# Reading the moving columns of the feed-forward products alternately from the left and the right half

## The chip, the core and the metric

The kernel runs on one core of one Trainium2 chip. The metric is the device time of one launch in microseconds (us); of the kernel before there are three runs, with a median of 897.61 us (897.53 to 898.24). Beside these times there is one profiled execution, whose trace is read below. All arithmetic happens on the core; the host only lays the input arrays out.

## The reference

Eight sequences of 576 tokens with eight heads of 64 features go through an attention that looks only inside chunks of 64 tokens. The result, 4608 tokens by 512 features, goes through a gated feed-forward part with 1536 hidden features:

```python
def _attn_ref(q, k, v):                       # each (8, 8, 576, 64), chunk = 64
    scores = scale * np.matmul(q_c, k_c.transpose(0, 1, 2, 4, 3))
    scores = scores - np.max(scores, axis=-1, keepdims=True)
    attn = np.exp(scores)
    attn = attn / (np.sum(attn, axis=-1, keepdims=True) + 1e-09)
    out = np.matmul(attn, v_c)

def _moe_ref(x, w_gate, w_val, w_out):        # x (4608, 512)
    g = x @ w_gate                            # (512, 1536)
    silu = g * (1.0 / (1.0 + np.exp(-g)))
    val = x @ w_val
    return (silu * val @ w_out).astype(np.float32)
```

Tokens are independent of each other in the feed-forward part: whatever order the 4608 rows are worked in, each gives the same row of the output.

## The kernel before

**Tiling.** The 4608 tokens are worked in 9 groups of 512 (`N`), the 512 input features in 4 blocks of 128 (`NK`), the 1536 hidden features in 12 blocks `f` of 128 (`NF`). A group's attention output lies in SBUF with features on the 128 partitions and the 512 tokens along each partition. So the products of the feed-forward part all have one shape. A weight block of 128 x 128 is loaded into the TensorE array, and 512 columns are streamed past it into one PSUM bank. The streamed operand is called the moving operand here. In the gate and value products it is a group's tokens (`x`, `xh`, `xl`); in the output product (`project`) the array holds 128 hidden-layer tokens and the moving operand is the 512 columns of a block of the output weights (`both`, `two`).

**Precision.** Each float32 factor is split in an upper and a lower part, both of the type float32r (names ending in h or hi, and l or lo), by a cast on ScalarE and a subtraction on VectorE (`split`, L62 and L63). Each product is then three matmuls: lower times upper, upper times lower, upper times upper. The weights arrive as 64-bit floats and are narrowed on the chip (`class Narrow`): a ScalarE instruction reads the high 32-bit words of the pairs (L80), another the low words (L87), so both step by two words. `class Out` does this for the output weights, 512 columns per block `f`.

**Order of the work.** Groups 0 and 1 come first, together with the narrowing of the weights. Their blocks 0 to 5 are plain products (`some`, L475); the later blocks combine two groups in a scheme of seven products instead of eight (`seventh`, L863). The narrowed weights and their sums are written to device memory on the way. Group 2 follows with plain products. Groups 3 and 4, 5 and 6, 7 and 8 are then worked in pairs with seven products per block (`gated_pair`), reading the weights back from device memory block after block. The gated hidden block `h` is split again and multiplied by the output weights (`project`, L538 to L540), which adds up in four PSUM banks, one per 128 tokens, over all 12 blocks. After the last block, ScalarE scales each bank into `o_sb` and a DMA on SP's queue writes the 128 rows to the output (L553, L554). The order of instructions on TensorE, ScalarE and VectorE is that of the program text (`manual_schedule`); attention steps of later groups are put between the feed-forward steps by tables of callbacks (`middle`, `behind`, `bursts`).

**Operand addresses.** Every moving operand of the lines L475, L538 to L540 and L863 is a run of 512 consecutive 4-byte words in each partition. One other line streams 512 columns: L664, which subtracts the row maxima from the scores of the first two groups. Its moving operand is a short row of maxima, each repeated 64 times:

```python
nc.tensor.matmul(ps, minus, top[:, h].broadcast_to(list(ps.shape)), start=False, stop=True,
                 skip_group_check=True)
```

Of the kernel before, what the change touches and what calls it, by code (L numbers as in the profile page):

```python
# [8 lines left out]
F32 = mybir.dt.float32  # L9
F32R = mybir.dt.float32r  # L10
U32 = mybir.dt.uint32
I32 = mybir.dt.int32
U64 = mybir.dt.uint64
AF = mybir.ActivationFunctionType
# [3 lines left out]
P = 128  # L18
C = 64
B, H, S, D = 8, 8, 576, 64  # L20
NT = B * S
# [5 lines left out]
T = 4  # L27
N = T * P
NB = NT // N
# [4 lines left out]
def attn_then_gated_ffn(ctx: ExitStack, tc: tile.TileContext, qk, v, wgv, wo, out):  # L34
    nc = tc.nc
# [15 lines left out]
    minus = const.tile([P, P], F32R, name="minus")  # L51
    nc.scalar.activation(minus, ident, AF.Copy, scale=-1.0)

    def keep_warm(n):

        ps = ps_gv.tile([P, P], F32, name="unread", tag="ps_gv")
        for _ in range(n):
            nc.tensor.transpose(ps, ident, ident)
# [6 lines left out]

    w_hi, w_lo, wo_raw, w_both = [], [], [], []

    class Narrow:


# [6 lines left out]


        def scale(self):
            nc.scalar.activation(self.t, self.high.bitcast(F32), AF.Prelu, scale=2.0 ** -111, alpha=2.0 ** 32)  # L80

        def shift(self):
            nc.vector.tensor_scalar(out=self.ti, in0=self.ti, scalar1=3, scalar2=None, op0=ALU.logical_shift_left)


        def below(self):
            nc.scalar.activation(self.units, self.low.bitcast(U32), AF.Copy, scale=2.0 ** -29)  # L87

        def join(self):
            nc.vector.tensor_tensor(out=self.ti, in0=self.ti, in1=self.units, op=ALU.add)  # L90
# [84 lines left out]
    def moved(i):  # L175
        return f"w{(i + EARLY) % NF}"
# [47 lines left out]
    class Out(Narrow):  # L224
# [14 lines left out]
        def scale(self):  # L239
            wo_raw.append(const.tile([P, 2, DM], F32, name="wo", tag=f"wo{self.f % 2}")[:, 0])  # L240
            super().__init__(self.mine, wo_raw[self.f], hp.tile([P, DM], F32, name="o_sb", tag="o_sb"))
            super().scale()


# [226 lines left out]
    def some(ps, a, f, g, which, first=True, last=True):  # L471
        for k, i in which:
            w = (w_hi, w_lo, w_hi)[i][f][:, g, k]
            x = a.x[k // 2][i == 0][:, k % 2]
            nc.tensor.matmul(ps, w, x, start=first and (k, i) == which[0], stop=last and (k, i) == which[-1])  # L475

    def out_weights(f):
        both = wp.tile([P, 2, DM], F32R, name="both", tag="wo")
        split(wo_raw[f], both[:, 0], both[:, 1])
        if f % 2 == 0:  # L480
            o = store.tile([P, 2, 2, DM], F32, name=f"o{f}")
            kept_o[f], kept_o[f + 1], two_o[f // 2] = o[:, 0], o[:, 1], o
        out_now[f] = both
        return both[:, 0], both[:, 1]
# [6 lines left out]
    def out_again(f, pool=wp, tag="wo"):  # L491
        both = pool.tile([P, 2, DM], F32R, name="both", tag=tag)
        recent[:] = [nc.sync.dma_start(out=both.bitcast(F32), in_=kept_o[f]).ins]
        return both[:, 0], both[:, 1]
# [7 lines left out]
    def product(a, f, g):  # L502
        ps = ps_gv.tile([P, N], F32, name="ps_gv")
        some(ps, a, f, g, IN_TURN)
        return ps
# [24 lines left out]
        return a, f, hh, hl  # L530

    def project(parts, wo_f, which=range(T)):
        (a, f, hh, hl), (woh, wol) = parts, wo_f
        if not hasattr(a, "o"):
            a.o = [ps_o.tile([P, DM], F32, name="ps_o") for _ in range(T)]
        for t in which:
            ts, o = slice(t * P, (t + 1) * P), a.o[t]
            nc.tensor.matmul(o, hl[:, ts], woh, start=f == a.steps[0], stop=False)  # L538
            nc.tensor.matmul(o, hh[:, ts], wol, start=False, stop=False)  # L539
            nc.tensor.matmul(o, hh[:, ts], woh, start=False, stop=f == a.steps[1])  # L540
            if f == a.steps[1]:

                pool, tag = (hp, "o_sb") if t % 2 == 0 else (ld, "v_t")
                o_sb = pool.tile([P, DM], F32, name="o_sb", tag=tag)
                r = a.b * N + t * P

                halves = 2 if r + P == NT else 1
                for i in range(halves):
                    m = slice(i * DM // halves, (i + 1) * DM // halves)
                    if i:  # L550
                        nc.vector.tensor_scalar_mul(o_sb[:, m], o[:, m], 2.0 ** -8)
                    else:
                        nc.scalar.activation(o_sb[:, m], o[:, m], AF.Copy, scale=2.0 ** -8)  # L553
                    nc.sync.dma_start(out=out[r:r + P, m], in_=o_sb[:, m])  # L554

    pending = []

    def lag(parts, wo_f):

        if pending:  # L560
            project(*pending.pop())
        if parts is not None:
            pending.append((parts, wo_f))
# [21 lines left out]
    w, o = up[0], down[0]  # L585
# [36 lines left out]
    class Product:  # L622
# [4 lines left out]
        def add(self, *which):  # L627
            for w in which:
                self.left -= 1
                some(self.ps, *self.at, [w], first=self.left == 3 * NK - 1, last=not self.left)  # L630
# [68 lines left out]
    for a, qs in ((a0, q0[0] + q0[1]), (a1, q1[0] + q1[1])):  # L699
# [16 lines left out]
        L13 w1u  # L716
    """
    keep_warm(15)
    for do in opening.split():
        if do[0] == ".":  # L720
            keep_warm(int(do[1:]))
        elif do[0] in "gvw":
            getattr(weights[do[:-1]], steps[do[-1]])()
        elif do[0] in "GV":
            if do[0] not in products:
                products[do[0]] = Product(a0, 0, "GV".index(do[0]))
            products[do[0]].add((int(do[3]), int(do[4])))
        elif do[0] == "e":
            a0.exchange(v0[int(do[1])][:, 1], values[int(do[1])][1], nc.scalar.copy)
        elif do == "H0":  # L730
            h0 = silu(products["G"].ps)
        elif do == "Q0":
            times(h0, products["V"].ps)
        else:
            b, i = int(do[1]), int(do[2])
            pairs = do[0] in "STCUL"
            getattr(couples[b, i // 2 if pairs else i], do[0])(i if pairs else int(do[3:] or 0))
# [4 lines left out]
    w = up[1]  # L742
# [16 lines left out]
    wo_f = out_weights(0)  # L759
# [52 lines left out]
    for f in range(1, SEVEN):  # L812
        w, o = up[f + 1], down[f]
# [32 lines left out]
        wo_f = out_weights(f)  # L846
# [11 lines left out]
    def seventh(ps, x, factors, i, first):  # L858
        which, q = FACTORS[i]
        w = [t.rearrange("p (i k m) -> p i k m", i=4, m=P)[:, q] for t in factors[which]]  # L860
        for k in range(NK // 2):
            for n, (u, v) in enumerate(((0, 1), (1, 0), (0, 0))):
                nc.tensor.matmul(ps, w[u][:, k], x[i][v][:, k], start=first and k == 0 and n == 0,  # L863
                                 stop=k == NK // 2 - 1 and n == 2, skip_group_check=True)

    def add(t, ps):
# [2 lines left out]
    def turns(which):  # L869

        if pending:
            project(*pending[0], which=which)
            if T - 1 in which:
                pending.pop()

    def first_seven(f, done, before):
# [11 lines left out]
        def product(ps, i, first):  # L888
            seventh(ps, x_first, factors, i, first)
# [92 lines left out]
    wo_f = pending[0][1]  # L982
# [140 lines left out]
    def gated_pair(pair, f, h2, inside, middle):  # L1123
# [9 lines left out]
        v12 = const.tile([P, 2, N], F32, name="v", tag=("ts", "wo1")[f % 2])  # L1133
        v1, v2 = v12[:, 0], v12[:, 1]
        seventh(ps1, pair.x, loaded[f], 0, True)
        nc.scalar.copy(out=h, in_=ps1)
        seventh(ps2, pair.x, loaded[f], 1, True)
        nc.scalar.copy(out=v2, in_=ps2)
        turn_of(0)
# [71 lines left out]
    a, pair = nxt, []  # L1211
# [44 lines left out]
    for i in range(NF):  # L1256
        f = (i + EARLY) % NF
        h = gated(a, f)
        middle.get(i, lambda: None)()
        wo_f = out_again(f)  # L1260
# [13 lines left out]
    for b in range(3, NB, 2):  # L1274
        pair.last = b + 2 == NB
        middle, behind, bursts, later = {}, {}, {}, {}
        if not pair.last:
            n = Pair(b + 2, moved(11))
# [46 lines left out]
```

## Time and profile before

| what | value |
|---|---|
| device time, median of 3 runs | 897.61 us |
| span of the profiled execution | 895.6 us |
| TensorE matmuls in it (PE) | 6047, of which 3636 have 128 x 512 on lines L475, L538 to L540, L863 |
| busy share of PE, VectorE (DVE), ScalarE (ACT) | 99%, 61%, 43% |
| mean traffic of the DMA engines | 249 GB/s |

The span runs from the first to the last instruction of the profiled execution; the device time has some 2 us more. "PE" rows are matmuls, "PEld" rows the loads of the array, which overlap matmuls. A matmul's duration in the trace reaches from its first column to the end of its passage through the array, and the next matmul starts before that end; so the pace of a chain of matmuls is the distance of their starts, not their mean duration. A row such as "1.36 PE ps_a L863 x6" in the chain of waits gives the time of six matmuls on the path. The granted clock is the share of TensorE's full clock that the throttle let through.

### The profile page before, as it was taken

Reading aid. Unit: us, or ns where it says so; the run is one execution under the profiler, and the core shown is the slowest. Engines: PE = TensorE matmul, PEld = TensorE weight load, DVE = VectorE, ACT = ScalarE, POOL = GpSimd, SP = SyncE. Lnnn points to the kernel's source line nnn. Section 1 sums busy time; section 2 is a strip of 40 time slices with the busy share of each in tenths; the row PEclk is TensorE's granted clock in tenths of the full one; section 3 lists DMA queues with packets and bytes.
Section 4 is the critical chain, followed back from the end, with each engine's and each line's share of the span. In section 5 each row is a group of like instructions: output and inputs, shape, how many; then the busy total and the mean of one; then the engine's idle time right before and its main releaser. Section 6 shows DMA issues by size and latency. Waiting matters only on the chain.

```text
span 895.6 us, 14752 instructions
## 1 busy us (share of the span) xinstructions
PE 884.2 (99%) x6047; PEld 732.2 (82%) x6047; DVE 546.6 (61%) x834; ACT 386.6 (43%) x587; POOL 17.1 (2%) x18
## 2 busy tenths in 40 slices
PE   7999999999999999999999999999999999999998
PEld 6788888878888888888888888888888888888886
DVE  5889999673787555776753756766645533333332
ACT  5856677543533335334334444234335432223232
POOL 1200000000021000000000000000000000000000
PEclk9999999999999999999999999999999999999999
DMA  9688776899899566666587857566657565556651
GB/s 355 258 305 327 293 287 233 315 310 340 299 363 291 188 235 224 246 235 213 211 282 250 301 208 270 217 235 221 208 230 270 188 259 197 195 209 233 235 188 47
DMA packets 73170, 223.25 MB, mean 249 GB/s; under 512 B 30736, under 2 KB 30992, under 8 KB 58896
## 3 DMA queue, kind: packets, MB, share of 16 engines
q1 hardware_dynamic: 71664, 219.70, 67.7%
q10 hardware_dynamic: 1440, 2.62, 0.9%
q8 instruction: 47, 0.77, 0.3%
q14 instruction: 19, 0.16, 0.0%
HBM read 178.78 MB, written 43.52 MB: 248 GB/s over the span
## 4 chain that ended last, share of the span: by engine, by line
PE 94%; DVE 2%; DMA 2%; POOL 0%; ACT 0%; issue 0%; SPq 0%; DVEq 0%; POOLq 0%
PE ps_a L863 26%; PE ps_gv L863 19%; PE ps_gv L475 13%; PE ps_o L538 11%; PE ps_o L540 11%; PE ps_o L539 11%; PE ps_a L287 2%; DMA v_t<-in_v 2%; DVE turned L352 1%; PE ps_a L365 1%; DMA qk_t<-in_qk 1%; PE ps_a L465 0%; POOL v_t L408 0%; DVE h L519 0%; PE ps_a L451 0%
## 5 line engine op out<-in xcount | busy, mean ns | idle before, releaser
L863 PE MATMUL ps_a<-x,factors 128*128 128x512 f32 x864 | 219.2, 389 | 0.0
L863 PEld LDWEIGHTS ps_a<-x,factors 128*128 128x128 f32 x864 | 162.2, 188 | 33.7
L863 PE MATMUL ps_gv<-x,factors 128*128 128x512 f32 x648 | 164.4, 389 | 0.0
L863 PEld LDWEIGHTS ps_gv<-x,factors 128*128 128x128 f32 x648 | 121.6, 188 | 25.2
L538 PE MATMUL ps_o<-both,hl 128*128 128x512 f32 x336 | 132.2, 394 | 0.2 <-DVE hl L63 0.2
L540 PE MATMUL ps_o<-both,hh 128*128 128x512 f32 x336 | 130.8, 389 | 0.0
L539 PE MATMUL ps_o<-both,hh 128*128 128x512 f32 x336 | 130.8, 389 | 0.0
L475 PE MATMUL ps_gv<-xh,w 128*128 128x512 f32 x384 | 116.9, 390 | 0.2 <-ACT xh L614 0.2
L63 DVE TENSOR_TENSOR hl<-h,hh 128x512 fp32r<-128x512 f32 x98 | 67.9, 692 | 61.8 <-ACT hh L62 61.6
L62 ACT CAST hh<-h 128x512 fp32r<-128x512 f32 x98 | 60.6, 618 | 97.3 <-PE ps_o L540 51.3
L867 DVE TENSOR_TENSOR h<-h,ps_gv 128x512 f32<-128x512 f32 x42 | 28.8, 686 | 105.7 <-PE ps_gv L863 105.5
L352 DVE STREAM_TRANSPOSE turned<-s_sb 32x256 f32<-32x256 f32 x192 | 83.7, 436 | 2.7
L475 PEld LDWEIGHTS ps_gv<-xh,w 128*128 128x128 f32 x384 | 72.0, 188 | 15.8 <-issue 0.7
L519 DVE SCALAR_TENSOR_TENSOR h<-v,h 128x512 f32<-128x512 f32 x84 | 58.1, 692 | 38.0 <-ACT h L1159 33.0
L538 PEld LDWEIGHTS ps_o<-both,hl 128*128 128x128 f32 x336 | 63.1, 188 | 14.1 <-DVE hl L63 0.7
L475 PE MATMUL ps_gv<-xl,w 128*128 128x512 f32 x192 | 73.4, 392 | 0.8 <-ACT s_sb L368 0.8
L540 PEld LDWEIGHTS ps_o<-both,hh 128*128 128x128 f32 x336 | 63.1, 188 | 13.3
L539 PEld LDWEIGHTS ps_o<-both,hh 128*128 128x128 f32 x336 | 63.1, 188 | 12.7
L1159 ACT ACTIVATE h<-ps_a 128x512 f32<-128x512 f32 x36 | 21.5, 598 | 112.2 <-PE ps_a L863 112.2
L867 DVE TENSOR_TENSOR v<-v,ps_a 128x512 f32<-128x512 f32 x42 | 28.9, 688 | 41.1 <-PE ps_a L863 36.4
L1145 ACT ACTIVATE h<-h 128x512 f32<-128x512 f32 x36 | 22.8, 632 | 52.9 <-DVE h L867 52.9
L867 DVE TENSOR_TENSOR v<-v,ps_gv 128x512 f32<-128x512 f32 x42 | 28.9, 688 | 24.5 <-PE ps_gv L863 24.2
(132 smaller groups left out, 1015.1 us busy)
## 6 DMA issues: line engine op xcount, KB each, us to landing
factors<-w SPq DMA_DIRECT2D x36, 1024.0 KB, 4.8
factors<-t SPq DMA_DIRECT2D x36, 1024.0 KB, 5.9
both<-o SPq DMA_DIRECT2D x70, 512.0 KB, 6.2
w<-w SPq DMA_DIRECT2D x16, 1024.0 KB, 7.9
t<-th SPq DMA_DIRECT2D x24, 512.0 KB, 3.7
two<-o SPq DMA_DIRECT2D x12, 1024.0 KB, 5.1
raw<-in_wgv SPq DMA_DIRECT2D x11, 1024.0 KB, 8.8
qk_t<-in_qk SPq DMA_DIRECT2D x10, 1024.0 KB, 8.5
```

Of the source, the lines that this page charges most:

```text
L62: nc.scalar.copy(out=hi, in_=src)
L63: (engine or nc.vector).tensor_tensor(out=lo, in0=src, in1=hi.bitcast(F32), op=ALU.subtract)
L352: nc.vector.transpose(out=self.turned[to:to + 32, p:p + 2, j, :, 32 * (i % 2):32 * (i % 2) + 32], in_=src[32 * i:32 * i + 32, :, o // 2, 3 ...
L475: nc.tensor.matmul(ps, w, x, start=first and (k, i) == which[0], stop=last and (k, i) == which[-1])
L519: nc.vector.scalar_tensor_tensor(out=h, in0=pv, scalar=2.0 ** -8, in1=h, op0=ALU.mult, op1=ALU.mult)
L538: nc.tensor.matmul(o, hl[:, ts], woh, start=f == a.steps[0], stop=False)
L539: nc.tensor.matmul(o, hh[:, ts], wol, start=False, stop=False)
L540: nc.tensor.matmul(o, hh[:, ts], woh, start=False, stop=f == a.steps[1])
L863: nc.tensor.matmul(ps, w[u][:, k], x[i][v][:, k], start=first and k == 0 and n == 0, stop=k == NK // 2 - 1 and n == 2, skip_group_check=True)
L867: nc.vector.tensor_tensor(out=t, in0=t, in1=ps, op=ALU.add)
L1145: nc.scalar.activation(h, h, AF.Silu, scale=2.0 ** -8)
L1159: nc.scalar.activation(h2, ps1, AF.Silu, scale=2.0 ** -8)
```

## The change

A helper gives a view of the moving operand whose column 2b is column b of the left half (of 256) and whose column 2b + 1 is column b of the right half. Every matmul of `some`, `seventh` and `project` now streams its 512 columns in this order: word 0, word 256, word 1, word 257, and so on. The number of matmuls, the weights that they load and the order of all instructions on TensorE, ScalarE and VectorE stay the same.

On SP's queue, which a scheduler orders, something moves at four places, each at the end of a token group: a load of output weights for a later block is now queued behind four writes of output rows instead of two. At the end of the group of token rows 1536 to 2047 the queue had, before (`out` is the output, `o_sb` the scaled rows, `both` a block of output weights, `factors` the two halves of a block's gate and value weights):

```order
L493 DMA both<-o_1575 128x1024
L554 DMA out<-o_sb 128x512 x2
L493 DMA both<-o_1794 128x1024
L554 DMA out<-o_sb 128x512 x2
L1120 DMA factors<-w_661 128x2048
```

and has now:

```order
L504 DMA both<-o_1575 128x1024
L565 DMA out<-o_sb 64x2x512 x4
L504 DMA both<-o_1794 128x1024
L1131 DMA factors<-w_661 128x2048
```

The second load of `both` has moved behind the third and fourth write of output rows. That block of output weights is the eleventh of the twelve that the next group multiplies with.

The results would come out permuted, and two edits put that right. For the gate and value products it is the tokens that are permuted: position 2b + a of a hidden block now belongs to token 256a + b. Nothing depends on the order until the rows are written, so only the DMA of the output rows gets a view that sends them to their places: 128 rows of 512 words as before, in a pattern of 64 x 2 rows. For the output product it is the output columns that are permuted; the block of output weights is therefore laid out the other way round when it is narrowed: `Out.scale` reads the even columns into the left half and the odd ones into the right half, so its two ScalarE instructions per block read with a step of four words instead of two. They write as many words as before.

```diff
+    def in_turn(x):
+        return x.rearrange("p (a b) -> p b a", a=2)
...
+    def as_shaped(t, like):
+        return t if len(like.shape) == 2 else t.rearrange("p (a b) -> p a b", b=like.shape[2])
...
         def scale(self):
-            nc.scalar.activation(self.t, self.high.bitcast(F32), AF.Prelu, scale=2.0 ** -111, alpha=2.0 ** 32)
+            nc.scalar.activation(as_shaped(self.t, self.high), self.high.bitcast(F32), AF.Prelu, scale=2.0 ** -111,
+                                 alpha=2.0 ** 32)
...
         def below(self):
-            nc.scalar.activation(self.units, self.low.bitcast(U32), AF.Copy, scale=2.0 ** -29)
+            nc.scalar.activation(as_shaped(self.units, self.low), self.low.bitcast(U32), AF.Copy, scale=2.0 ** -29)
...
             super().__init__(self.mine, wo_raw[self.f], hp.tile([P, DM], F32, name="o_sb", tag="o_sb"))
+            self.low, self.high = (w.rearrange("p (b a) -> p a b", a=2) for w in (self.low, self.high))
             super().scale()
...
-            nc.tensor.matmul(ps, w, x, start=first and (k, i) == which[0], stop=last and (k, i) == which[-1])
+            nc.tensor.matmul(ps, w, in_turn(x), start=first and (k, i) == which[0],
+                             stop=last and (k, i) == which[-1])
...
     def project(parts, wo_f, which=range(T)):
-        (a, f, hh, hl), (woh, wol) = parts, wo_f
+        (a, f, hh, hl), (woh, wol) = parts, map(in_turn, wo_f)
...
-                r = a.b * N + t * P
-                halves = 2 if r + P == NT else 1
+                rows = out[a.b * N:(a.b + 1) * N].rearrange("(a b) m -> b a m", a=2)[t * P // 2:(t + 1) * P // 2]
+                halves = 2 if (a.b, t) == (NB - 1, T - 1) else 1
...
-                    nc.sync.dma_start(out=out[r:r + P, m], in_=o_sb[:, m])
+                    nc.sync.dma_start(out=rows[:, :, m], in_=o_sb[:, m])
...
-                nc.tensor.matmul(ps, w[u][:, k], x[i][v][:, k], start=first and k == 0 and n == 0,
+                nc.tensor.matmul(ps, w[u][:, k], in_turn(x[i][v][:, k]), start=first and k == 0 and n == 0,
                                  stop=k == NK // 2 - 1 and n == 2, skip_group_check=True)
```

## The prediction

> **What bounds the kernel now.** First the clock and the busy shares, then the chain of waits, then the pace of the matmuls.
>
> ```profile
> core 0: 895.6 us, clock 1.000
> PE 884.2 (99%) x6047; PEld 732.2 (82%) x6047; DVE 546.6 (61%) x834; ACT 386.6 (43%) x587; POOL 17.1 (2%) x18
> PE 94%; DVE 2%; DMA 2%; POOL 0%; ACT 0%; issue 0%; SPq 0%; DVEq 0%; POOLq 0%
> ```
>
> The granted clock is full throughout, so a throttle plays no part. TensorE is busy for 884.2 of 895.6 us, and 94% of the chain that ended last is its matmuls. Whatever changes the time of a matmul changes the end, for as long as the other engines keep up. The chain of waits also shows the pace: six matmuls of one accumulation stand in it as one row.
>
> ```profile
> 410.21 1.36 PE ps_a L863 x6
> L863 PE MATMUL ps_a<-x,factors x864: 389/389/393, 332.0 to 855.6; 128*128 128x512 f32 x173
> L863 PE MATMUL ps_gv<-x,factors x648: 389/389/389, 333.3 to 852.8; 128*128 128x512 f32 x162
> L538 PE MATMUL ps_o<-two,hl x96: 389/389/389, 490.9 to 880.3; 128*128 128x512 f32 x96
> L475 PE MATMUL ps_gv<-xh,w x384: 387/389/499, 26.1 to 329.0; 128*128 128x512 f32 x192
> 700.00:800.00 100.00, 100.00 (x442) 82.83 (x442) 35.59 (x50) 32.25 (x54) 0.00 (x0) 1.00 0.59 219
> ```
>
> 1.36 us for six is 226.7 ns from start to start. The rows below (from the views of single lines: minimum, median and maximum of a duration in ns) show one duration, 389 ns, for every tile that is streamed: tokens, hidden sums, output weights. The stretch from 700 to 800 us holds 442 matmuls, which is 226 ns for each, with no gap. So the price is a property of the stream, not of an address or a neighbour. The change touches all matmuls of L475 (576), L538 to L540 (1296) and L863 (1764): 3636 in all, or 3636 x 0.2267 = 824 us of the 895.6.
>
> **Is there anything to gain on a matmul?** One line streams 512 columns in another way: L664, whose moving operand is eight words, each repeated 64 times.
>
> ```profile
> L664 PE MATMUL ps_a<-tops,minus x16: 379/379/483, 8.3 to 25.9; 128*128 128x512 f32 x16
> L664 PEld LDWEIGHTS ps_a<-tops,minus x16: 186/189/189, 8.3 to 25.7; 128*128 128x128 f32 x16
> 25.14 0.70 PE L664 MATMUL ps_a<-tops,minus 128*128 128x512 f32 x2
> 25.14 1.13 PE L664 MATMUL ps_a<-tops,minus 128*128 128x512 f32 x4
> L863 PEld LDWEIGHTS ps_a<-x,factors x864: 187/188/188, 331.7 to 855.3; 128*128 128x128 f32 x173
> ```
>
> Its matmuls take 379 ns, 10 less than all others. The two timeline rows give the pace: two of them end 0.70 us after the start, four 1.13 us after it, so two more cost 0.43 us, 215 ns each. The load of the array is the same in both lines (188 and 189 ns), so it is not the load that makes up the 11 to 12 ns between 226.7 and 215. What differs is how many fresh words must be fetched: 512 from consecutive addresses, or eight. I read this as a small stall in the fetch of a fast run of new words, one that every one of the 3636 matmuls pays. That stall is what the change can remove, and there is no more than it to gain.
>
> Does reading in turn remove it? The change makes two runs of the one, and each run now advances at half the pace. The nearest row for a slower advance is the transposes:
>
> ```profile
> 205.88 1.91 PE L451 MATMUL pt<-ident,s_sb 128*128 128x128 f32 x16
> L451 PE MATMUL pt<-ident,s_sb x16: 270/272/273, 205.9 to 207.5; 128*128 128x128 f32 x16
> ```
>
> Sixteen take 1.91 us; less the last one's 0.272 us that is 109 ns from start to start, or 0.85 ns for each of 128 columns, against 0.443 ns (226.7/512) in the products. Twice the pace of L664 would be 0.84 ns per column (2 x 215/512), twice the pace of the products 0.89. So at half the pace the stall is all but gone, as far as another kind of matmul can tell. If the fetch works ahead in each run by itself, then two runs at half pace each should show no stall either. If instead it works ahead only along one run, every column is a jump. No row of this trace has a product whose next word lies in another place, so the price has to be bounded from both sides.
>
> **The sum.** Per matmul, the best that the rows allow is the pace of L664, 215 to 216 ns (by the two timeline rows, and by 226.7 less the 10 ns of duration, 216.7). I take 216: 10.7 ns saved, x 3636 = 38.9 us. The bounds are 10 ns (36.4 us) and 11.7 ns (42.5 us); the worse side is for the rivals.
>
> What the faster TensorE uncovers must be taken off again:
>
> ```profile
> 60.00:160.00 100.00, 100.00 (x443) 82.71 (x442) 92.36 (x126) 69.69 (x96) 0.00 (x0) 1.00 0.75 280
> 180.00:280.00 100.00, 98.69 (x1030) 81.38 (x1030) 67.39 (x108) 42.12 (x61) 5.50 (x4) 1.00 0.93 326
> 400.00:895.00 495.00, 492.03 (x2995) 407.31 (x2993) 250.02 (x379) 181.82 (x289) 0.00 (x0) 1.00 0.61 221
> ```
>
> The columns are PE, PEld, DVE, ACT and POOL busy, then the granted clock, the DMA engines' busy share and GB/s. Between 60 and 160 us, VectorE is busy for 92.36 of 100 us while it narrows and splits weights. At 216 ns the stretch shrinks to 95.3 us, which leaves VectorE 3% of slack in a strict order of work. I take 2 us off the 4.7 won there (bounds 0 and 4.7). Between 180 and 280 us the DMA engines are busy for 0.93 of the time, and 0.97 of the shrunken one; I take 1 us off (bounds 0 and the whole 4.7). From 400 us on, nothing but TensorE is near its limit: VectorE has 250 of 495 us, the DMA engines 0.61.
>
> The side effects. The order of TensorE, ScalarE and VectorE is the same, so no wait is added there. The 24 ScalarE instructions of the output weights read with a step of four words instead of two:
>
> ```profile
> L62 ACT CAST both<-wo x12: 603/615/623, 41.5 to 179.1; 128x512 fp32r<-128x512 f32 x12
> L80 ACT ACTIVATE wo<-raw x12: 648/662/695, 38.3 to 167.6; 128x512 f32<-128x512 f32 x12
> L80 ACT ACTIVATE t<-raw 128x1024 f32<-128x1024 f32 x11 | 12.6, 1147 | 0.0
> L162 ACT CAST th<-ts 128x1024 fp32r<-128x1024 f32 x11 | 11.6, 1053 | 1.2 <-ACT h L512 0.8 <-DVE ts L150 0.2 <-DMA t<-th 0.2
> ```
>
> A step of two words costs ScalarE 662 instead of 615 ns for 512 words. For twice the step the bounds are nothing, and a doubling of the 0.94 ns per word ((1147 - 662)/512): 24 x 0.48 = 11.6 us of ScalarE, spread over 38 to 172 us, where it is busy for 70%. That is hidden; without cover it would cost up to 11.6 us. I take 0. The rows of the output go out in as many pieces of 2 KB as before, and the four loads of output weights that move behind two more writes on SP's queue are needed ten blocks of 12 matmuls later, about 27 us: 0.
>
> Span: 895.6 - 38.9 + 3 = 859.7 us; the runs' median stands 2.0 us above the span, so the forecast is **861.7 us**.
>
> **The rivals.**
>
> 1. *Every column a jump: slower.* The fetch brings neighbouring words together, and in turn only one word of each fetch is used. For it: ScalarE pays for taking every second word, 0.94 ns per word against 0.86 ((1053 - 615)/512) for consecutive ones, so the words that are fetched and not used do cost; and the 0.443 ns that a product allows per column is half of either. The place is the stream of all 3636 matmuls, and it decides as soon as a separate word takes longer than 0.443 ns. At the transposes' 0.85 ns per column a matmul takes 436 ns: + 209 ns x 3636 = 761 us, about 1,660 us. At ScalarE's 0.94 ns it is 483 ns, + 932 us, about 1,830 us. Against it: those rows are of slower engines or of work that is bound by its own pace, and none shows that two interleaved runs can't be fetched ahead. [...]
>
> 2. *The stall stays: no change.* It may belong to every so many bytes, whatever order they are read in, or to something else in which L664 differs (its array holds the same block each time). Then the pace stays 226.7 ns and the time 897.6 us. For it: the same 389 ns everywhere fits a fixed fee as well.
>
> 3. *Another engine takes the gain.* VectorE's and the DMA engines' stretches give up all of their 4.7 us: 897.6 - 38.9 + 9.4 = 868.1 us. Still faster; it widens the range.
>
> **How the numbers follow.** The stall is real and large enough to see, and the only row at half pace is free of it, which speaks for the gain. What speaks against is a cost that no row here excludes and that would be large. I give the forecast 0.54 and rival 3 0.10, together 0.64 for faster; no change (rival 2) 0.16; and a loss 0.20, of which 0.17 for rival 1, far above 1,000 us, and 0.03 for a stall that grows a little. A measurement of this kernel can tell about 0.2%, 1.8 us, from no change. The range goes from the full 11.7 ns with nothing given back (897.6 - 42.5 = 855) over rival 3 and the unchanged time to a small loss of 2 ns per matmul (905); it leaves out rival 1 and little else.
>
> **What would show it.** The duration of the products, 389 ns now: 379 and a pace of 216 ns in L475, L538 to L540 and L863 alike if I am right, 389 for rival 2, well over 500 for rival 1, with TensorE busy all the same. The 24 instructions of the output weights at 662 ns or more tell what ScalarE thinks of the wider step. If the pace falls and the time does not follow, the stretches 60 to 160 and 180 to 280 us must show new idle time on TensorE ahead of VectorE's results or DMAs. I am wrong if the products slow down, or if they differ among the three places: then the address, not the order, counts.

## The result, and the profile after

The changed kernel takes 868.65 us (median, 868.55 to 869.0) against 897.92 us before in the same session: 0.9675 of the time, 95% interval 0.9661 to 0.9689, or 29.3 us less. The forecast was 861.7 us, 36 us less. The profiled execution has a span of 866.8 us.

The page of the changed kernel (busy times and shares, then the shares of the chain that ended last):

```profile
PE 847.8 (98%) x6047; PEld 736.0 (85%) x6047; DVE 545.9 (63%) x834; ACT 413.6 (48%) x587; POOL 17.0 (2%) x18
PE 78%; DVE 11%; ACT 5%; DMA 2%; issue 2%; POOL 1%; SPq 0%; ACTq 0%; DVEq 0%; POOLq 0%
```

TensorE is busy for 36 us less. ScalarE (ACT), whose work has not changed in number, is busy for 27 us more. And the chain is no longer TensorE's alone: VectorE and ScalarE now hold 16% of it.

The products, in the views of single lines (minimum, median, maximum in ns) and in the chain of waits:

```profile
L874 PE MATMUL ps_gv<-x,factors x648: 379/379/379, 329.4 to 825.2; 128*128 128x512 f32 x162
L549 PE MATMUL ps_o<-two,hl x96: 379/379/379, 479.9 to 851.4; 128*128 128x512 f32 x96
L485 PE MATMUL ps_gv<-xh,w x384: 378/379/483, 26.6 to 325.3; 128*128 128x512 f32 x192
508.51 1.29 PE ps_a L874 x6
```

All three places went from 389 to 379 ns, and six matmuls on the path from 1.36 to 1.29 us, 215 ns each by this rounded row. By the starts in the traces themselves, products of one accumulation are 226.8 ns apart before and 216.0 ns after. That is the duration and pace of the one line that streamed eight repeated words before.

The stretches that the prediction named, after (PE, PEld, DVE and ACT busy, POOL, granted clock, share of the DMA engines, GB/s):

```profile
60.00:160.00 100.00, 96.13 (x436) 81.35 (x435) 91.31 (x124) 87.35 (x93) 0.00 (x0) 1.00 0.71 272
180.00:280.00 100.00, 97.69 (x1046) 84.78 (x1045) 68.67 (x112) 43.58 (x63) 6.11 (x5) 1.00 0.95 337
400.00:860.00 460.00, 459.93 (x2921) 402.26 (x2912) 245.23 (x371) 176.74 (x281) 0.00 (x0) 1.00 0.64 234
```

From 60 to 160 us TensorE now does 436 matmuls where it did 443, with 3.9 us of idle time that was not there. ScalarE went from 69.69 to 87.35 us of the 100. From 400 us on nothing waits.

TensorE's instructions come in the same order in all kernels here, so the start of the same matmul can be compared. The table is worked out from the traces: by how many us each stretch of the kernel before (by its own times) has become shorter (-) or longer (+). "Full" is 10.8 ns (226.8 less 216.0) for each product in the stretch. The rows below the first two are the experiments of the next section.

```
                          0-40   40-180   180-280   280-890
full                      -0.4    -6.6      -4.0     -28.0
the change                +0.3    +1.5      -3.2     -28.0
e1 weights laid out       +0.2    -2.4      -3.0     -28.2
e2 in turn from group 2   +0.2     0.0      -1.3     -28.2
e5 reads in halves        -0.1    -3.8      -2.4     -28.2
e6 without joins          +0.1    -5.9      -2.0     -28.2
e8 64 words apart         +0.1    -2.4      -2.2     -28.1
e11 four and four         -0.2    -3.6      -2.3     -28.2
e12 neither               -0.4    -6.8      -2.5     -28.2
```

Each row comes from one execution. e1 and e8 have the same pace and the same ScalarE reads; they agree from 40 to 180 us but differ by 0.8 us from 180 to 280 us, so differences of that size in the third column say little.

After 280 us the gain is whole; three of the four loads of output weights that moved on SP's queue lie there, so they cost nothing. (The fourth, at 234 us, was not measured by itself.) Between 40 and 180 us, while the weights are narrowed, the gain is not only lost: the stretch got 1.5 us longer, 8.1 us short of the full gain. The same stretch by the clock, before and then after, and the two longest waits of TensorE's matmuls in it after the change (who waited, for whom, us in total, times, longest):

```profile
40.00:180.00 140.00, 140.00 (x619) 115.81 (x618) 122.24 (x171) 92.69 (x129) 0.00 (x0) 1.00 0.79 294
40.00:180.00 140.00, 134.93 (x612) 114.38 (x611) 121.73 (x170) 118.95 (x129) 0.00 (x0) 1.00 0.76 288
PE ps_a L874 <- ACT h L913: 3.2, 5, 1.1
PE ps_gv L485 <- DVE h L530: 1.3, 3, 0.7
```

TensorE now idles for 5.1 us, 3.2 of them ahead of a ScalarE instruction (L913), and ScalarE is busy for 119 us where it was busy for 93. The 24 reads of the output weights stand out there, and so do other reads whose operands the change does not touch. First three rows of before, then after:

```profile
L87 ACT ACTIVATE t<-raw 128x1024 int32<-128x1024 uint32 x11 | 12.6, 1143 | 0.0
L87 ACT ACTIVATE o_sb<-raw 128x512 int32<-128x512 uint32 x12 | 8.0, 665 | 0.0
L80 ACT ACTIVATE wo<-raw 128x512 f32<-128x512 f32 x12 | 8.0, 664 | 0.0
```

```profile
L87 ACT ACTIVATE wo<-raw x12: 1449/1563/1644, 38.9 to 170.0; 128x512 f32<-128x512 f32 x12
L87 ACT ACTIVATE t<-raw x13: 658/1580/1596, 7.5 to 157.6; 128x1024 f32<-128x1024 f32 x11, 128x512 f32<-128x512 f32 x2
L87 ACT ACTIVATE wo<-raw 128x512 f32<-128x512 f32 x12 | 18.8, 1563 | 0.0
L95 ACT ACTIVATE o_sb<-raw 128x512 int32<-128x512 uint32 x12 | 18.5, 1543 | 0.0
L95 ACT ACTIVATE t<-raw 128x1024 int32<-128x1024 uint32 x11 | 17.1, 1553 | 0.1
L87 ACT ACTIVATE t<-raw 128x1024 f32<-128x1024 f32 x11 | 17.0, 1544 | 0.0
```

The output weights (`wo`, `o_sb`), now read with a step of four words, went from 662 to 1563 ns. The other weights (`t`), still read with a step of two words, went from 1147 to 1544 ns. Together the four groups are 71.4 us of ScalarE, against 41.2 before (8.0 + 8.0 + 12.6 + 12.6).

### The profile page after: what moved, and what is told of

It is laid out like the page before. It is cut to its first block, busy times and chain, and to the rows that moved or that the text cites. A ratio compares the mean times of both kernels' runs of the same rounds, so it can differ in the third digit from the quotient of the medians.

```text
span 866.8 us, 14752 instructions
## 1 busy us (share of the span) xinstructions
PE 847.8 (98%) x6047; PEld 736.0 (85%) x6047; DVE 545.9 (63%) x834; ACT 413.6 (48%) x587; POOL 17.0 (2%) x18
## 4 chain that ended last, share of the span: by engine, by line
PE 78%; DVE 11%; ACT 5%; DMA 2%; issue 2%; POOL 1%; SPq 0%; ACTq 0%; DVEq 0%; POOLq 0%
PE ps_a L874 23%; PE ps_gv L874 17%; PE ps_o L549 10%; PE ps_o L551 9%; PE ps_o L550 9%; PE ps_gv L485 6%; DMA v_t<-in_v 2%; PE ps_a L297 2%; DVE turned L362 2%; PE ps_a L375 1%; DVE h L530 1%; DVE w L138 1%; DVE t L98 1%; ACT wo L87 1%; ACT t L87 1%
## 5 line engine op out<-in xcount | busy, mean ns | idle before, releaser
L874 PE MATMUL ps_a<-x,factors 128*128 128x512 f32 x864 | 210.0, 379 | 0.0
L874 PE MATMUL ps_gv<-x,factors 128*128 128x512 f32 x648 | 157.5, 379 | 0.0
L549 PE MATMUL ps_o<-both,hl 128*128 128x512 f32 x336 | 128.7, 383 | 0.4 <-DVE hl L67 0.4
L551 PE MATMUL ps_o<-both,hh 128*128 128x512 f32 x336 | 127.3, 379 | 0.1
L550 PE MATMUL ps_o<-both,hh 128*128 128x512 f32 x336 | 127.3, 379 | 0.0
L485 PE MATMUL ps_gv<-xh,w 128*128 128x512 f32 x384 | 112.8, 379 | 0.0
L66 ACT CAST hh<-h 128x512 fp32r<-128x512 f32 x98 | 60.3, 615 | 87.1 <-PE ps_o L551 47.4
L485 PEld LDWEIGHTS ps_gv<-xl,w 128*128 128x128 f32 x192 | 36.2, 189 | 9.1 <-DVE h L530 3.0
```

What stands on the lines that cost most here:

```text
L66: nc.scalar.copy(out=hi, in_=src)
L485: nc.tensor.matmul(ps, w, in_turn(x), start=first and (k, i) == which[0], stop=last and (k, i) == which[-1])
L874: nc.tensor.matmul(ps, w[u][:, k], in_turn(x[i][v][:, k]), start=first and k == 0 and n == 0, stop=k == NK // 2 - 1 and n == 2, skip_group ...
```

## The experiments

### Is it ScalarE's reads? The output weights laid out by the host (e1)

The host puts the columns of `w_out` in their new order, and `Out.scale` no longer does. Nothing else changes.

```diff
-            self.low, self.high = (w.rearrange("p (b a) -> p a b", a=2) for w in (self.low, self.high))
...
-    wo = np.ascontiguousarray(inputs["moe_w_out"])
+    wo = np.asarray(inputs["moe_w_out"])
+    wo = np.ascontiguousarray(wo.reshape(DF, DM // 2, 2).transpose(0, 2, 1).reshape(DF, DM))
```

> The output weights' columns are put in their new order when the host lays the array out, so ScalarE reads them with a step of two words again; all products still read in turn. Theory A (the 8 us that the stretch from 40 to 180 us loses come from ScalarE's strided reads, the 24 of the output weights at 1.55 instead of 0.66 us above all): these fall to 0.66 to 0.8 us, ScalarE is relieved of some 20 us, and the time falls by 4 to 7 us, to 862 to 865 us. Theory B (a faster TensorE simply runs into VectorE's 92% there, or into the DMAs): ScalarE is relieved but the time stays at 868 to 869 us.

Measured: 864.68 us, 0.9632 of before (0.9619 to 0.9646), faster than both kernels: its interval lies below that of the change.

```profile
L87 ACT ACTIVATE wo<-raw x12: 855/880/897, 38.8 to 166.6; 128x512 f32<-128x512 f32 x12
L87 ACT ACTIVATE t<-raw x13: 660/1555/1594, 7.2 to 154.6; 128x1024 f32<-128x1024 f32 x11, 128x512 f32<-128x512 f32 x2
40.00:180.00 140.00, 138.11 (x631) 117.86 (x630) 123.92 (x174) 105.11 (x130) 0.00 (x0) 1.00 0.79 299
```

The time is in the range of theory A, so the wider step, read beside products in turn, cost 4 us. But the reads of `wo` fell to 880 ns only, not to the 662 of before, though they are now the same instruction on the same kind of operand. And `t` stays slow.

### Do the products slow ScalarE's reads? In turn from group 2 on (e2)

On top of e1, the products of groups 0 and 1 read one column after the other; the rows of these groups are put right where ScalarE scales them.

```diff
-            nc.tensor.matmul(ps, w, in_turn(x), start=first and (k, i) == which[0],
+            nc.tensor.matmul(ps, w, in_turn(x) if a.b > 1 else x, start=first and (k, i) == which[0],
...
-        (a, f, hh, hl), (woh, wol) = parts, map(in_turn, wo_f)
+        (a, f, hh, hl), (woh, wol) = parts, map(in_turn, wo_f) if parts[0].b > 1 else wo_f
...
+                if a.b < 2:
+                    rows = out[a.b * N + t * P:a.b * N + (t + 1) * P]
+                    nc.scalar.activation(o_sb.rearrange("p (b a) -> p a b", a=2), o.rearrange("p (a b) -> p a b", a=2), AF.Copy, scale=2.0 ** -8)
...
+                part = x[i][v][:, k]
+                nc.tensor.matmul(ps, w[u][:, k], part if x is x_first else in_turn(part), start=first and k == 0 and n == 0,
```

> As the run before, but the products of groups 0 and 1, beside which the weights are narrowed, read their columns one after the other; the reading in turn begins with group 2, at about 190 us. Theory A with contention (ScalarE's reads with a step of two words, 1.58 instead of 1.14 us for 1024 words, are slowed by TensorE's reading in turn beside them): these reads are back at 1.14 us, TensorE has no idle time from 40 to 180 us, and the time is 897.9 less 10.8 ns for each of the some 2,600 later products, 869 to 871 us. If the reads stay at 1.58 us, something else than the order of reading slows them.

Measured: 869.21 us, 0.9686 of before (0.9673 to 0.9699), in the expected range.

```profile
L87 ACT ACTIVATE t<-raw x13: 660/1140/1182, 7.3 to 155.5; 128x1024 f32<-128x1024 f32 x11, 128x512 f32<-128x512 f32 x2
L87 ACT ACTIVATE wo<-raw x12: 642/662/677, 38.5 to 167.7; 128x512 f32<-128x512 f32 x12
40.00:180.00 140.00, 140.00 (x620) 115.77 (x619) 122.29 (x170) 92.54 (x129) 0.00 (x0) 1.00 0.79 292
```

Both reads are back at their old times as soon as TensorE reads one column after the other beside them. So it is TensorE's reading in turn that slows ScalarE's reads with a step. In e2 TensorE also has its old pace beside these reads; that the order counts and not the faster pace alone is shown by e11 below, where the products start every 215 ns and the reads of `t` take 1151 ns. Reads of consecutive words are not slowed: the cast of 512 words (L66, before the change L62; the mean of the 98 casts of `h`) takes 615 ns after the change and took 618 before.

### What does the wider step cost by itself? (e4)

The reverse: `in_turn` returns its operand unchanged and the rows go out as before the change; the output weights are read with the step of four.

```diff
     def in_turn(x):
-        return x.rearrange("p (a b) -> p b a", a=2)
+        return x
```

> The reverse: all products read one word after the other as before the change, but the output weights are read with a step of four words (the output's columns come out in another order). If the wider step alone costs ScalarE the time, its 24 reads last about 1.5 us here too; if they are slow only beside a TensorE that reads in turn, they last 0.66 to 0.75 us. The time is within 2 us of before in the second case, up to 5 us more in the first. Products: 389 ns.

Measured: 897.32 us in a single run.

```profile
L87 ACT ACTIVATE wo<-raw x12: 1105/1130/1170, 38.3 to 167.5; 128x512 f32<-128x512 f32 x12
L87 ACT ACTIVATE t<-raw x13: 658/1142/1202, 7.5 to 155.2; 128x1024 f32<-128x1024 f32 x11, 128x512 f32<-128x512 f32 x2
40.00:180.00 140.00, 140.00 (x619) 115.86 (x619) 122.11 (x171) 103.06 (x130) 0.00 (x0) 1.00 0.79 296
```

1130 ns is neither of the two expected numbers: the step alone costs 0.47 us per read, 11 us of ScalarE, and reading in turn beside it 0.43 us more. With e1 and e2 the four cases for 512 words of `wo` are complete: 662 ns with neither, 1130 with the step, 880 with the products in turn, 1563 with both. At the old pace of TensorE (389 ns a product) the step stays hidden; no time is lost (897.56 us before, in the same session).

### Do the places gain one by one? Gate and value products only (e3)

```diff
-        (a, f, hh, hl), (woh, wol) = parts, map(in_turn, wo_f)
+        (a, f, hh, hl), (woh, wol) = parts, wo_f
```

(and `Out.scale` no longer reorders the output weights; the host leaves them as they were, too).

> Gate and value products read in turn, the output products read their columns one after the other, the output weights are narrowed as before the change. If each product gains by itself: the gate and value products last 379 ns, the output products 389 ns, and the time is that of the first run of this call plus 1296 x 10.8 ns = 14 us less what the stretch of the narrowing takes back, 873 to 878 us. If the gain needs all products to read in turn, the durations are the same on all lines.

Measured: 879.69 us, 0.9801 of before (0.9788 to 0.9814), 15.0 us above e1. That is over the expected range of 873 to 878 us, but 14 us on top of the 864.68 of e1 would have been 878.7.

```profile
L548 PE MATMUL ps_o<-two,hl x96: 389/389/389, 481.5 to 861.1; 128*128 128x512 f32 x96
L873 PE MATMUL ps_gv<-x,factors x648: 379/379/379, 329.0 to 833.7; 128*128 128x512 f32 x162
```

Each product has the duration of its own operand's order: 379 ns in turn, 389 ns one after the other, side by side in one kernel.

### What takes the rest from 40 to 180 us? (e5, e6, e12)

In e1 that stretch still lacks 4.2 us. e5 takes ScalarE's steps away altogether, by reading as many consecutive words instead, with a copy in place of the first instruction; e6 leaves out 25 VectorE instructions; e12 does both.

```diff
# e5 and e12, on top of e1
-            words = raw.bitcast(I32).rearrange("p (n t) -> p n t", t=2)
-            self.low, self.high = words[:, :, 0], words[:, :, 1]
+            words = raw.bitcast(I32).rearrange("p (t n) -> p t n", t=2)
+            self.low, self.high = words[:, 0], words[:, 1]
# e6 and e12, on top of e1
         def join(self):
-            nc.vector.tensor_tensor(out=self.ti, in0=self.ti, in1=self.units, op=ALU.add)
+            pass
```

> As the first run (output weights laid out by the host, all products in turn), but ScalarE reads the 64-bit weights as two halves of consecutive words instead of every second word, as many words and instructions as before; the weights come out as zeros, so the output is zero. Theory A (what is still lost from 40 to 180 us, 4 us, comes from ScalarE's reads with a step, 1.54 us for 1024 words): these reads fall to 1.05 to 1.1 us and the time to 860 to 861.5 us. Theory B (VectorE's 92% limits the stretch): reads fall, time stays at 864 to 865 us.

> As the first run, but the 25 VectorE instructions that add the low bits to the narrowed weights (join) are left out, some 22 us of VectorE between 24 and 175 us; the weights are less exact. Theory A: ScalarE's reads stay at 1.54 us and the time at 864 to 865 us. Theory B: the time falls to 860 to 861.5 us.

> The first run with both reliefs: ScalarE reads the 64-bit weights in consecutive words and VectorE's 25 joins are left out (the weights come out as zeros). If ScalarE and VectorE together take the rest of the gain between 40 and 180 us, that stretch now gains its whole 6.6 us, TensorE has no idle time there, and the time is 858.5 to 860.5 us. If a third thing holds it back, such as the DMAs that bring the weights, it stays at 862 us or more.

Measured: e5 863.64 us (0.9626, 0.961 to 0.9641), e6 862.55 us (0.9609, 0.9593 to 0.9625), e12 861.08 us (0.9601, 0.9585 to 0.9617). The intervals of e1, e5 and e6 overlap; that of e12 lies below that of e1. The stretch from 40 to 180 us, with the reads of `t` in e5, tells more:

```profile
L87 ACT ACTIVATE t<-raw x13: 630/1052/1069, 7.2 to 153.2; 128x1024 int32<-128x1024 uint32 x11, 128x512 int32<-128x512 uint32 x2
40.00:180.00 140.00, 138.87 (x650) 119.13 (x653) 124.29 (x176) 90.84 (x132) 0.00 (x0) 1.00 0.80 301
```

And the same stretch in e6, then in e12:

```profile
40.00:180.00 140.00, 139.41 (x704) 121.57 (x703) 109.00 (x156) 106.10 (x134) 0.00 (x0) 1.00 0.82 311
```

```profile
40.00:180.00 140.00, 140.00 (x708) 122.41 (x707) 109.30 (x157) 91.68 (x135) 0.00 (x0) 1.00 0.83 312
```

Neither theory was right alone. With ScalarE relieved TensorE still idles for 1.1 us, beside a VectorE that is busy for 124 of 140 us; the stretch gains 1.4 us (table above). With VectorE relieved it gains 3.5 us. With both it gains 4.4 us, TensorE has no idle time, and the full 6.6 us are there. So of the 4.2 us that e1 lacked, VectorE holds the larger part and ScalarE's slowed reads the rest. e11 below says the same without leaving any work out: its products have the new pace, its ScalarE reads have their old times, and the stretch still lacks 3.0 us of the full gain.

```profile
40.00:180.00 140.00, 138.79 (x647) 118.63 (x649) 124.21 (x176) 93.36 (x132) 0.00 (x0) 1.00 0.80 301
```

The time of e12 is 0.6 us above its range, though: from 180 to 280 us it loses 1.5 us of its gain; the kernels that read in turn throughout lose 0.8 to 2.0 us there. That stretch was not tested further, and the cause of its loss stays open.

### Why does reading in turn help? Other orders (e7 to e11)

These are e1 with another view in `in_turn`; each changes the order of the columns and nothing else.

```diff
-        return x.rearrange("p (a b) -> p b a", a=2)
+        return x.rearrange("p (a b c) -> p b a c", a=2, c=2)    # e7: two words of each half in turn
+        return x.rearrange("p (o a b) -> p o b a", a=2, b=64)   # e8: two places 64 words apart
+        return x.rearrange("p (a b) -> p b a", a=4)             # e9: four quarters
+        return x.rearrange("p (o a b) -> p o b a", a=2, b=2)    # e10: 0, 2, 1, 3
+        return x.rearrange("p (o a b) -> p o b a", a=2, b=4)    # e11: 0, 4, 1, 5, 2, 6, 3, 7
```

> As the first run, but the products read two neighbouring words of the left half and two of the right half in turn (the output comes out in another order). If the gain comes from two runs that are fetched ahead each by itself, the products last 379 ns as in turn word by word. [...] If ScalarE's reads with a step suffer from the number of separate fetches of TensorE, they fall from 1.54 towards 1.34 us.

> As the first run, but the two places that are read in turn lie 64 words apart instead of 256 (four blocks of 128 columns, each of two halves; the output comes out in another order). Two runs that are fetched ahead: 379 ns. [...]

> As the first run, but the products take one word from each of four quarters in turn (the output comes out in another order). Theory C (any number of runs is fetched ahead, each by itself): 379 ns, as in turn between two halves; but pairs of words at 502 ns already speak against it. Theory D (words in even and odd places of the stream are fetched by two lanes, each holding one line of four words; a lane that needs a new line for each word loses time, as with pairs, and for every second word a little, as one word after the other; with the halves in turn each lane runs along its own half): the even lane alternates between two quarters, a new line for each word, so about 502 ns, a pace of 333 ns.

> As the first run, but in each group of four words the order is 0, 2, 1, 3 (the output comes out in another order). Theory C: two runs in turn, 379 ns. Theory D: each lane takes two words of a line and then a new line, as with consecutive words, so 389 ns and a pace of 227 ns, though no word follows its neighbour.

> As the first run, but in each group of eight words the order is 0, 4, 1, 5, 2, 6, 3, 7 (the output comes out in another order). Theory D: each lane takes all four words of a line (if lines are 16 bytes and the operands start on one), so 379 ns and a pace of 216 ns, with no two runs far apart at all. If lines have nothing to do with it and the two places must lie further apart, 389 ns or more.

64 words apart (e8): the products in the view of their line and in the chain of waits, then ScalarE's reads:

```profile
L873 PE MATMUL ps_gv<-x,factors x648: 379/379/379, 326.3 to 821.9; 128*128 128x512 f32 x162
604.64 1.29 PE ps_gv L873 x6
L87 ACT ACTIVATE t<-raw x13: 666/1560/1597, 7.3 to 154.5; 128x1024 f32<-128x1024 f32 x11, 128x512 f32<-128x512 f32 x2
```

Pairs (e7), the products in the view of their line and in the chain of waits:

```profile
L873 PE MATMUL ps_gv<-x,factors x648: 502/502/503, 464.3 to 1218.7; 128*128 128x512 f32 x162
599.88 2.00 PE ps_gv L873 x6
```

Quarters (e9):

```profile
L873 PE MATMUL ps_gv<-x,factors x648: 448/448/448, 401.2 to 1045.1; 128*128 128x512 f32 x162
634.65 1.70 PE ps_gv L873 x6
```

Two and two (e10):

```profile
L873 PE MATMUL ps_gv<-x,factors x648: 389/389/395, 333.3 to 853.2; 128*128 128x512 f32 x162
600.33 1.36 PE ps_gv L873 x6
```

Four and four (e11), with ScalarE's reads:

```profile
L873 PE MATMUL ps_gv<-x,factors x648: 379/379/379, 324.7 to 820.3; 128*128 128x512 f32 x162
602.99 1.29 PE ps_gv L873 x6
L87 ACT ACTIVATE t<-raw x13: 660/1147/1197, 7.2 to 153.2; 128x1024 f32<-128x1024 f32 x11, 128x512 f32<-128x512 f32 x2
```

All orders together (duration of a product in ns; its pace, a sixth of the row of six, in ns; ScalarE's mean for 1024 words with a step of two, in ns; time in us, one run each but for the first two rows):

| order of the words | duration | pace | ScalarE's read | time |
|---|---|---|---|---|
| one after the other (before) | 389 | 227 | 1147 | 897.6 |
| halves in turn (e1) | 379 | 215 | 1531 | 864.68 |
| 64 words apart (e8) | 379 | 215 | 1536 | 865.55 |
| four words apart (e11) | 379 | 215 | 1151 | 863.65 |
| two words apart (e10) | 389 | 227 | 1150 | 898.37 |
| pairs from two halves (e7) | 502 | 333 | 1162 | 1281.94 |
| four quarters (e9) | 448 | 283 | 1150 | 1099.82 |

Theory C, that each run is fetched ahead by itself, falls with e7: two runs, advancing at half the pace just as in the change, cost 502 ns instead of 379. ScalarE's reads, expected to fall towards 1.34 us if they suffer from the number of TensorE's separate fetches, fell further, to 1162 ns; but TensorE's pace is much slower there as well (333 ns). e8 shows that the distance doesn't matter to TensorE down to 64 words: 379 ns and a pace of 215 ns, as with 256.

Theory D, a supposition of mine, does better: two lanes, one for the even and one for the odd places of the stream, each with one line of four words. It told the durations of e10 and e11 to the nanosecond before they ran. In e10 no word follows its neighbour and nothing is gained (389 ns); in e11 the two places are 16 bytes apart and everything is (379 ns). It told the loss of e9 but not its size: by theory D e7 and e9 should cost the same, since in both each lane meets a new line at every word, but they measured 333 and 283 ns. So theory D sorts every order tried into gain, no change and loss; what a lane pays when it changes lines with each word is not settled, and that there are such lanes inside, or lines of four words, is not shown.

## Why the prediction was right, and where not

**What bounds the kernel, and the size of the gain per matmul: right.** 389 ns became 379 and 226.7 became 215 to 216 ns, on all three lines, as the one row with repeated words had promised. From 280 us on the table has 28.0 us of 28.0. The full gain over all products is 39 us (38.9 in the prediction's sum). The time alone would be weak evidence, since the range of 855 to 905 us held the unchanged time too; it is the durations and the table that show the gain.

**The reason given for it: wrong.** "If the fetch works ahead in each run by itself, then two runs at half pace each should show no stall either": e7 and e9 are runs at half pace and less, and they are slower than before the change. The transposes, from which I argued, said nothing about this: each of them brings its own load of the array (L451 has 16 loads of 140 ns beside its 16 matmuls), so their 0.85 ns per column need not be a pace of the fetch at all. That reading in turn helped was luck as far as the reason goes: of the orders with two runs at half pace, the one chosen gains and pairs lose. If theory D holds, it gains because it happens to give each lane its own run.

**Rival 1, every column a jump: not here,** but it was no idle rival. Pairs cost 384 us, and a change with hardly another view would have met it. Its price was too high: 333 ns was the worst of the orders tried, where I had 436 to 483 (485, with ScalarE's 0.947 ns per word not cut short to 0.94). That the fetch brings neighbouring words together, as this rival supposes, no run shows; what the runs show is a pace of 333 ns for pairs and 283 ns for quarters, against 227 ns for one word after the other.

**The side effect on ScalarE: the step that failed.** "For twice the step the bounds are nothing, and a doubling of the 0.94 ns per word ...: 24 x 0.48 = 11.6 us of ScalarE ... I take 0." The upper bound was right for the step alone (e4: 11 us of ScalarE, hidden). But TensorE's new order of reading slows every read with a step beside it, which no row of the kernel before could show: ScalarE's four groups of reads rose by 30 us (the 24 reads of the output weights by 21, the others by 9), not by 11.6, in the stretch where the prediction also took away the cover, by a faster TensorE. It cost 4 us of time (the change against e1), plus the smaller part of the 4.2 us that e1 still lacks.

**The give-back.** I took 2 us for VectorE's stretch and 1 us for the DMAs'; the measured loss is 8.1 us from 40 to 180 us, 0.8 us from 180 to 280 us and 0.7 us before 40 us. Of the 8.1, some 3 us are what the faster TensorE uncovers beside a ScalarE at its old speed (3.0 in e11; e12 against e5 puts it on VectorE), near the 2 I took; the other 5 are ScalarE's slowed reads. The 9.6 us of loss instead of 3 make up nearly all of the 7 us by which the forecast was too low. Rival 3 (868.1 us) had the time almost exactly, but for VectorE's and the DMAs' sake, not ScalarE's: its number was right by luck.

**The signs named beforehand** showed it only in part. TensorE has new idle time from 60 to 160 us, but 2.9 us of its 3.8 us of matmul waits there are for ScalarE, and none for a DMA; the prediction had named VectorE's results or DMAs. The 24 reads, "662 ns or more", stand at 1563.

## What to carry to other kernels

A row that does the same amount of work in another way (here 512 columns from eight repeated words, 379 ns against 389) prices a stall that all other rows share and none shows. When an operand's order is changed, every other engine that reads beside it belongs in the sum, above all those with little slack in the same stretch (here ScalarE's reads of 1024 words went from 1147 to 1544 ns); price the pair, not each alone. Try the neighbouring orders before building on one: an order with the same gain on TensorE that leaves ScalarE's reads alone (e11: 379 ns, and 1151 ns for the reads) was one index away, and so was a loss of 384 us. e11 as run gives its output in another order, with the output weights laid out by the host; a kernel that puts its own results right in that order was not tried.

## What the runs showed of the hardware

- A product of 512 float32r columns starts every 227 ns when the moving words are consecutive and every 215 to 216 ns when two places 16 bytes, 256 bytes or 1 KB apart are read in turn (8 bytes apart it stays at 227); in pairs from two places it takes 333 ns, from four places in turn 283 ns.
- TensorE's reading in turn slows ScalarE's reads with a step: 1024 words with a step of two from 1147 to about 1540 ns, 512 words with a step of two from 662 to 880 ns, with a step of four from 1130 to 1563 ns. It does so with the two places 256 bytes or 1 KB apart, not with 16 bytes (1151 ns), nor with the slower orders (1150 and 1162 ns). Why the distance matters to ScalarE and not to TensorE stays open.
- Beside products that read one word after the other, ScalarE reads 512 words in 662 ns with a step of two and in 1130 ns with a step of four; a cast of 512 consecutive words takes 615 ns.
